# Cosformer attention and a Hyena gate on one core: transposes by DMA, x2 in row tiles of 128, column tiles for the 64-row leftovers

## The chip, the cores and the metric

The kernel runs on one core of a Trainium2 chip. The metric is device time in microseconds (us), the median of several runs. One more execution is profiled; its span, its waits and its durations are what the text below calls the profile.

## The reference

Eight batches, 8 heads, 576 positions (S), 64 features a head; 8 x 64 = 512 channels (DM). All inputs and the output are float32.

```python
# attention: q, k, v are [8, 8, 576, 64]
theta = pi / 2 * arange(576) / 576
phi(x) = concat([relu(x) * cos(theta), relu(x) * sin(theta)], axis=-1)      # 128 features
kv  = einsum('bhsf,bhsd->bhfd', phi(k), v);  z = phi(k).sum(axis=2)
att = einsum('bhsf,bhfd->bhsd', phi(q), kv) / (phi(q) . z + 1e-6)
x   = att, heads side by side: [8, 576, 512]
# gate
x1, x2, x3 = split(x @ w_proj, 3)                      # w_proj [512, 1536]
conv = irfft(rfft(x2, axis=1) * rfft(filter, axis=0))  # along the 576 positions
out  = (x1 * conv * x3) @ w_out                        # [8, 576, 512]
```

## The kernel before

Everything between HBM and PSUM is f16. A load converts while it transfers (issued on GpSimd's queue, POOL): q, k and v arrive as `raw` tiles of 96 partitions, each partition holding six neighbouring positions of all heads; four `raw` buffers take turns. One set of names per batch:

- `emit_phi` (L460, the arithmetic through the helpers at L97 and L99): kp = relu(k) times cos and sin, 12 VectorE operations; qp = relu(q) and relu(q) times tan, 7 operations. The missing cos of a row cancels in the quotient; `epsc` corrects the 1e-6.
- `emit_va` (L125): v into a padded tile, 4 ScalarE copies. `emit_kv` (L485): 48 matmuls, phi(k) as weights.
- `emit_qt` (L499): 48 transposes of 96x96 on TensorE with a permutation matrix `perm`, which brings positions into the order of the later DFT; each PSUM unit is copied into `qpt` twice, forward by VectorE (L511) and backward by ScalarE (L515), as 60 of 64 columns. There is one `qpt` buffer.
- `emit_num` (L520): per head five matmuls of 128 rows (positions from the front in one half, mirrored from the back in the other), a reciprocal, and `att` [128, 5, 512] (L540).
- `emit_fx` (L547): a small matrix `fm` (24 blocks of 10 columns) folds `att` into `fx` [128 channels, 4, 24, 48]. Blocks 0 to 11 are the butterflies of a radix-6 step, blocks 12 to 23 the plain positions, both with channels on partitions. Sixteen matmuls of 240 columns (L556) and four of 192 for the leftover tile (L570).
- `emit_x2` (L584): 3 parts x 2 components x 4 matmuls of 512 columns with 96 rows each, evicted to `x2f` (L598). `emit_dft` (L600): six matmuls with the tables `tre` and `tim` (96x96), then the product with the filter's spectrum on VectorE (L612 to L617).
- `emit_gate` (L619): x1 and x3 directly from the plain blocks of `fx`, 64 matmuls of 288 columns (L630); x1 is evicted by ScalarE (L636), and VectorE multiplies it with x3 from PSUM into `g` (L638).
- `emit_inv` (L647): 32 inverse-DFT matmuls. `emit_y` (L665): additions and the product with g. `emit_out` (L684): five row tiles of 128 (the last from row 448, so 64 rows are computed twice), 20 matmuls of 512 columns (L695), eviction (L700, in the last batch L702 and L97), 9 stores on SyncE's queue (SP), part of them on ScalarE's in the last two batches.

Batches overlap by hand: turn b of the main loop (L801) holds x2, dft, gate and inv of batch b, num and fx of batch b+1, the loads, phi, va, qt and kv of batch b+2, and out of batch b-1. Batches 0 and 1 and the tables (DFT, filter spectrum) are set up ahead of the loop. Each engine takes its instructions in a fixed order, which a scheduler makes from the order of the calls; `with behind(...)` (L109) puts an engine's instructions behind a marked one. All PSUM work shares four units of [128, 2, 512] float32 (L63).

Of the kernel before, what the change touches and what calls it, by code (L numbers as in the profile page):

```python
# [17 lines left out]
def kernel(  # L18
# [15 lines left out]

    nc = tc.nc
# [6 lines left out]
    NT = 5  # L42
# [25 lines left out]
    tcol = consts.tile([128, NJ], FP32, tag="tcol", name="tcol")  # L68
    epsc = consts.tile([128, NT], FP32, tag="epsc", name="epsc")
    perm = consts.tile([NP, NP], FP16, tag="perm", name="perm")  # L70
# [5 lines left out]
    fm = consts.tile([128, 24, 10], FP16, tag="fm", name="fm")  # L76
    tre = consts.tile([NP, 3, NP], FP16, tag="tre", name="tre")
    tim = consts.tile([NP, 3, NP], FP16, tag="tim", name="tim")

# [9 lines left out]
    qpt_buf = [consts.tile([128, NH, NT, 2, 64], FP16, tag=f"qpt{i}", name=f"qpt{i}") for i in range(1)]  # L89
# [24 lines left out]
    raw_t = {}  # L114

    def load_qk(b, nm, hs=slice(0, NH)):
        src = {"q": q, "k": k, "v": v}[nm]
        if hs.start == 0:
            rw = work.tile([NP, NH, NJ * D], FP16, tag="raw", bufs=4, name=f"{nm}raw{b}")
            raw_t[(b, nm)] = rw  # L120
        nc.gpsimd.dma_start(
            out=raw_t[(b, nm)][:, hs], in_=src[b, hs].rearrange("h (p j) d -> p h (j d)", j=NJ)
        )

    def emit_va(b, xs=range(4)):  # L125
        for x in xs:
            hs = slice(2 * x, 2 * x + 2)
            nc.scalar.copy(  # L128
                out=va_buf[b % 2][:, hs, :, 0:D],
                in_=raw_t[(b, "v")][:, hs].rearrange("p h (j d) -> p h j d", j=NJ),  # L130
            )
# [28 lines left out]
    def emit_iotas(part):  # L160
# [13 lines left out]
        iota("sr_i", [NP, QS], lambda t: [(t, [[2, 3], [12, NP // 2]], 1, 0)])  # L174

    def emit_cols():
# [6 lines left out]
        nc.vector.memset(warm, 0.0)  # L183
        sj = cc["s6_i"]
# [3 lines left out]
        nc.vector.tensor_tensor(out=tcol, in0=tcol, in1=scol, op=AL.mult)  # L188

        u16 = small("u16p")  # L190
        rnd(u16, p, 1.0 / 16.0, -15.0 / 32.0)
        dest = small("dest")
        tsc(dest, p, 6.0, AL.mult)
        nc.vector.scalar_tensor_tensor(
            out=dest, in0=u16, scalar=-95.0, in1=dest, op0=AL.mult, op1=AL.add
        )
        tsc(perm, cc["nrow_i"], dest[0:NP], AL.is_equal)

    def emit_pads():
        for va in va_buf:  # L200
            nc.vector.memset(va[:, :, :, D : D + 2], 1.0 / A1)
        for t in qpt_buf:
            nc.vector.memset(t[:, :, :, 0, 60:64], 0.0)
            nc.vector.memset(t[:, :, :, 1, 0:4], 0.0)

    def emit_fm():

        p = cc["p"]
        loc = small("loc")
        side = small("side")  # L210
        nc.vector.tensor_copy(out=loc[0:64], in_=p[0:64])
        tsc(loc[64:128], p[64:128], -1.0, AL.mult, 127.0, AL.add)
        nc.vector.memset(side[0:64], 1.0)
        nc.vector.memset(side[64:128], -1.0)
        lo = small("lo")
        rnd(lo, loc, 1.0 / 6.0, -5.0 / 12.0)
        li = small("li")
        nc.vector.scalar_tensor_tensor(
            out=li, in0=lo, scalar=-6.0, in1=loc, op0=AL.mult, op1=AL.add
        )  # L220


        orb = small("orb", NT)
        for t in range(NT):
            tsc(orb[:, t : t + 1], lo, 10.0 * t, AL.add)
        oj = small("oj", NT)
        rnd(oj, orb, 1.0 / 16.0, -15.0 / 32.0)
        pos = small("pos", NT)

        tsc(pos, orb, 6.0, AL.mult)  # L230
        nc.vector.scalar_tensor_tensor(
            out=pos, in0=oj, scalar=-95.0, in1=pos, op0=AL.mult, op1=AL.add
        )
        nc.vector.scalar_tensor_tensor(
            out=pos, in0=li.to_broadcast([128, NT]), scalar=96.0, in1=pos, op0=AL.mult, op1=AL.add
        )
# [6 lines left out]
        orow_i = cc["orow_i"][:, 0:10]  # L243
        match = small("match", 10)
# [5 lines left out]
        for sl, (kk, c0) in enumerate([(0, 0.25), (3, 0.25), (1, 0.25), (1, 0.0), (2, 0.25), (2, 0.0)]):  # L250
# [4 lines left out]
        nc.scalar.activation(out=coef[:, 0:6], in_=ph, func=AF.Sin, scale=TWO_PI)  # L255
        tsc(coef[:, 3:6:2], coef[:, 3:6:2], 1.0 / R3, AL.mult)

        tsc(coef[:, 0:6], coef[:, 0:6], 2.0, AL.mult)
        tsc(coef[:, 0:6], coef[:, 0:6], RC, AL.add, -RC, AL.add)
        tsc(coef[:, 0:6], coef[:, 0:6], 0.5, AL.mult)  # L260
        tsc(coef[:, 6:12], coef[:, 0:6], side, AL.mult)
# [12 lines left out]
            in0=coef.unsqueeze(2).to_broadcast([128, 24, 10]),  # L274
            in1=match.unsqueeze(1).to_broadcast([128, 24, 10]),
# [23 lines left out]
    def emit_rows():  # L299
# [5 lines left out]
        par = cc["par"] = small("par")  # L305
        rnd(par, p, 0.5, -0.25)
        nc.vector.scalar_tensor_tensor(
            out=par, in0=par, scalar=-2.0, in1=p, op0=AL.mult, op1=AL.add
        )
# [10 lines left out]
    def emit_fwd_tables():  # L320
# [4 lines left out]
        u = small("u16")  # L325
        rnd(u, p, 1.0 / 16.0, -15.0 / 32.0)
        j = small("jr")
        nc.vector.scalar_tensor_tensor(
            out=j, in0=half, scalar=-3.0, in1=u, op0=AL.mult, op1=AL.add
        )  # L330
        w = small("w2s")

        tsc(w, p, 12.0, AL.mult, 1.0, AL.add)
        nc.vector.scalar_tensor_tensor(out=w, in0=u, scalar=-192.0, in1=w, op0=AL.mult, op1=AL.add)
        nc.vector.scalar_tensor_tensor(out=w, in0=j, scalar=2.0, in1=w, op0=AL.mult, op1=AL.add)
# [24 lines left out]
        for tb in (tre, tim):  # L360
            tsc(tb[:, 1:3], tb[:, 1:3], amp[0:NP], AL.mult)
            nc.vector.tensor_tensor(out=tb[:, 0], in0=tb[:, 0], in1=mask, op=AL.mult)

# [59 lines left out]
    def emit_h():  # L423
        hc, hs_, hb, alt = cc["hc"], cc["hs"], cc["hb"], cc["alt"]
        fa = filt16.rearrange("p x (j n) -> p x j n", j=3)
        for x, op in ((0, AL.add), (1, AL.subtract)):
# [5 lines left out]
        for bl in range(3):  # L432
# [15 lines left out]
            tsc(h3[:, bl, 1], u[0:NP, 1], sc, AL.mult)  # L448
            nc.vector.tensor_copy(out=h3[:, bl, 2], in_=h3[:, bl, 1])
        u = unit("h_nyq")  # L450
        for j in range(3):
            nc.tensor.matmul(
                u[0:1, 0], alt[:, j % 2 : j % 2 + 1], feo[:, 0, j], start=(j == 0), stop=(j == 2)
            )
        nc.scalar.activation(out=h3[0:1, 0, 2], in_=u[0:1, 0], func=AF.Copy, scale=1.0 / S)
# [4 lines left out]
    def emit_phi(b, nm, h0=0, nh=NH):  # L460
        rw = raw_t[(b, nm)]
        dst = kp_t if nm == "k" else qp_t
        if h0 == 0:
            dst[b] = work.tile([NP, NJ, NH, 2, D], FP16, tag=f"{nm}p", bufs=2 if nm == "q" else 1, name=f"{nm}p{b}")
        t = dst[b]
        if nm == "q":

            tsc(
                t[:, :, h0 : h0 + nh, 0],
                rw[:, h0 : h0 + nh].rearrange("p h (j d) -> p j h d", j=NJ), 0.0, AL.max,  # L470
            )
        for j in range(NJ):
            for cs, col in ((0, ccol), (1, scol)) if nm == "k" else ((1, tcol),):
                mark["phi", b, nm] = tsc(
                    t[:, j, h0 : h0 + nh, cs], rw[:, h0 : h0 + nh, ds(j * D, D)],
                    col[0:NP, j : j + 1], AL.mult, 0.0, AL.max,
                )
# [21 lines left out]
    def emit_qt(b, hp):  # L499
        qp, qpt = qp_t[b], qpt_buf[0]  # L500
        u = psum.tile([128, 2, 1024], FP16, tag="u", bufs=4, name=f"qt{b}_{hp}")
        for hh in range(2):
            for j in range(NJ):
                nc.tensor.transpose(  # L504
                    u[:, hh, ds(j * NP, NP)],
                    qp[:, j, 2 * hp + hh].rearrange("p a b -> p (a b)"),
                    perm,
                )
        hsl = slice(2 * hp, 2 * hp + 2)
        ev = nc.scalar.copy if b == 0 and hp < 2 else nc.vector.tensor_copy  # L510
        mark["qpt", b, hp] = ev(  # L511
            out=qpt[:, hsl, :, 0, 0:60],
            in_=u[:, :, 0:300].rearrange("p h (t c) -> p h t c", c=60),
        )
        nc.scalar.copy(  # L515
            out=qpt[:, hsl, ::-1, 1, 4:64],
            in_=u[:, :, 276:576].rearrange("p h (t c) -> p h t c", c=60),
        )

    def emit_num(b, hp, wm=0):  # L520
        qpt, kvs = qpt_buf[0], kvs_t[b]
        if hp == 0:
            att_t[b] = work.tile([128, NT, DM], FP16, tag="att", bufs=2, name=f"att{b}")
# [3 lines left out]
        for hh in range(2):  # L527
            h = 2 * hp + hh
            for t in range(NT):
                nc.tensor.matmul(  # L530
                    u[:, hh, ds(t * 65, 65)], qpt[:, h, t].rearrange("p a b -> p (a b)"),
                    kvs[:, h // 4, ds((h % 4) * 65, 65)], start=True, stop=True,
                )
        nv = u[:, :, 0 : NT * 65].rearrange("p h (t e) -> p h t e", e=65)
        rcp = work.tile([128, 2, NT], FP32, tag="rcp", bufs=2, name=f"rcp{b}_{hp}")
        nc.vector.tensor_tensor(
            out=rcp, in0=nv[:, :, :, 64], in1=epsc.unsqueeze(1).to_broadcast([128, 2, NT]), op=AL.add
# [5 lines left out]
            in1=rcp.unsqueeze(3).to_broadcast([128, 2, NT, D]),  # L543
# [3 lines left out]
    def emit_fx(b, cs=range(NC), ccs=None, wm=0):  # L547
        att = att_t[b]
        if 0 in cs:
            fx_t[b] = work.tile([128, NC, 24, 48], FP16, tag="fx", bufs=2, name=f"fx{b}")  # L550
        fx = fx_t[b]
        for c in cs:
            u = unit(f"fx{b}_{c}")
            warm_up(u, wm)
            for t in range(NT - 1):
                nc.tensor.matmul(  # L556
                    u[:, t // 2, 0:480].rearrange("p (g o) -> p g o", o=20)[:, :, ds((t % 2) * 10, 10)],
                    att[:, t, ds(c * 128, 128)], fm, start=True, stop=True,
                )
            nc.scalar.copy(  # L560
# [319 lines left out]
```

## Time and profile before

| | us |
|---|---|
| three runs | 269.84, 270.54, 272.35; median 270.54 |
| the profiled execution | 272.95 |
| its span | 271.2 |
| busy TensorE, VectorE, ScalarE | 243.0, 226.9, 196.8 |

Read it so: the span holds all engines at once, so a busy share near 100% means that an engine is hardly ever without work, and a part removed from another engine moves nothing unless it was waited for. TensorE's matmuls are pipelined, so one record (say 382 ns for 512 columns) is longer than the distance to the next (217 ns). The granted clock of TensorE was 0.978 of full speed on average; it was 0.5 between 66 and 70 us.

### The profile page before, as it was taken

What the parts mean: (1) busy time and instruction counts of PE and PEld (TensorE: products, weight loads), DVE (VectorE), ACT (ScalarE), POOL (GpSimd) and SP (SyncE); (2) the same over time, 40 slices, a digit from 0 to 9 for tenths busy, and PEclk for the clock granted to TensorE, in tenths of its full rate; (3) what the DMA queues carried; (4) which work ended last, traced back from release to release, by engine and by line L of the source; (5) the groups of instructions that cost most, each with busy time, mean ns of one, the idle gap of its engine ahead of it and who ended that gap; (6) DMA issues with size and microseconds to landing.
All of it is one profiled execution on the core that took longest, in us unless ns stands there. A gap on an engine that the chain in (4) does not pass through costs nothing.

```text
span 271.2 us, 6320 instructions
## 1 busy us (share of the span) xinstructions
PE 243.0 (90%) x2457; PEld 175.2 (65%) x2457; DVE 226.9 (84%) x805; ACT 196.8 (73%) x274; POOL 27.3 (10%) x47
## 2 busy tenths in 40 slices
PE   0287998878989999999999999999999999999991
PEld 0164767547858776786678676867687768756830
DVE  7689997998899898979897989978997479646951
ACT  2279679798497778877897789786977667857630
POOL 8551111020020101110111011000000000000000
PEclk9999999995799999999999999999999999999998
DMA  5999998919019296636860868114000600060235
GB/s 79 168 206 205 206 205 122 166 14 169 3 14 161 33 230 90 89 40 152 150 101 3 174 128 124 16 51 125 0 2 9 169 2 0 2 174 13 69 117 155
DMA packets 26991, 26.70 MB, mean 98 GB/s; under 512 B 1680, under 2 KB 22160, under 8 KB 26960
## 3 DMA queue, kind: packets, MB, share of 16 engines
q0 software_dynamic: 21200, 16.84, 42.7%
q1 hardware_dynamic: 5120, 8.39, 10.7%
q10 hardware_dynamic: 640, 1.05, 1.3%
q8 instruction: 19, 0.31, 0.5%
q14 instruction: 12, 0.10, 0.1%
HBM read 33.69 MB, written 9.44 MB: 159 GB/s over the span
## 4 chain that ended last, share of the span: by engine, by line
PE 50%; ACT 22%; DVE 21%; DMA 4%; issue 1%; POOL 0%; SPq 0%; POOLq 0%; ACTq 0%
PE x L630 20%; PE x L593 9%; ACT x2f L598 7%; ACT va L128 7%; PE kv L491 5%; PE out L695 4%; PE fx L556 4%; DVE eo L672 4%; ACT fx L560 3%; DMA vraw<-in_v_dram 2%; DVE kp L99 2%; PE qt L504 2%; PE dft L607 2%; PE inv L657 2%; DVE qpt L511 2%; PE inv L656 2%
## 5 line engine op out<-in xcount | busy, mean ns | idle before, releaser
L630 PE MATMUL x<-fx,wp 128*128 128x288 f16 x512 | 67.5, 286 | 1.1 <-ACT fx L560 1.0
L630 PEld LDWEIGHTS <-wp 128*128 128x128 f16 x512 | 50.0, 98 | 13.3 <-issue 0.3
L593 PE MATMUL x<-wp,fx 128*96 128x512 f16 x192 | 45.2, 382 | 0.5 <-ACT x2f L598 0.5
L560 ACT CAST fx<-fx 128x960 f16<-128x960 f32 x32 | 30.6, 961 | 13.7 <-PE fx L556 13.7
L695 PE MATMUL out<-wo,y 128*128 128x512 f16 x160 | 37.6, 379 | 0.7 <-DVE y L677 0.7
L598 ACT ACTIVATE x2f<-x 96x1024 f16<-96x1024 f32 x24 | 24.5, 1020 | 14.6 <-PE x L593 14.6
L593 PEld LDWEIGHTS <-fx 128*96 128x96 f16 x192 | 22.4, 124 | 15.1 <-issue 0.8
L672 DVE TENSOR_TENSOR eo<-eq 128x144 f16<-128x144 f16 x128 | 23.7, 228 | 10.1 <-ACT eq L660 9.9
L128 ACT COPY va<-vraw 96x768 f16<-96x768 f16 x32 | 25.3, 827 | 9.3 <-DMA vraw<-in_v_dram 9.3
L638 DVE TENSOR_TENSOR g<-x,x1s 128x288 f16<-128x288 f32 x64 | 27.0, 448 | 1.3 <-PE x L630 1.1
L491 PE MATMUL kv<-va,kp 96*128 96x65 f16 x384 | 16.4, 202 | 11.7 <-ACT va L128 8.8
L540 DVE TENSOR_TENSOR att<-num,rcp 128x640 f16<-128x640 f32 x32 | 26.1, 820 | 0.3
L515 ACT COPY qpt<-qt 128x600 f16<-128x600 f16 x32 | 20.4, 671 | 7.5 <-DVE qpt L511 7.5
L695 PEld LDWEIGHTS <-y 128*128 128x128 f16 x160 | 14.9, 97 | 16.0 <-DVE y L677 1.2
L609 ACT CAST xf<-dft 96x1024 f16<-96x1024 f32 x24 | 23.5, 1010 | 2.2 <-PE dft L607 1.2
L491 PEld LDWEIGHTS <-kp 96*128 96x128 f16 x384 | 15.3, 104 | 13.3 <-DVE kp L99 8.1
L504 PEld LDWEIGHTS <-qp 96*128 96x128 f16 x384 | 20.2, 102 | 5.1 <-issue 1.1
L636 ACT CAST x1s<-x 128x576 f16<-128x576 f32 x32 | 20.5, 639 | 4.2 <-PE x L630 3.1
L612 DVE TENSOR_TENSOR m<-xf,h 96x1024 f16<-96x1024 f16 x24 | 16.3, 678 | 7.8 <-ACT xf L609 7.7
L504 PE MATMUL qt<-perm,qp 96*128 96x96 f16 x384 | 21.7, 213 | 0.5 <-ACT fx L560 0.3
L700 ACT ACTIVATE os<-out 128x1024 f32<-128x1024 f32 (+1 forms) x21 | 18.3, 883 | 5.2 <-PE out L695 5.1
L556 PE MATMUL fx<-fm,att 128*128 128x240 f16 x128 | 18.8, 270 | 2.2 <-DVE att L540 1.1
(185 smaller groups left out, 419.4 us busy)
## 6 DMA issues: line engine op xcount, KB each, us to landing
out_dram<-os SPq DMA_DIRECT2D x22, 192.0 KB, 2.5
qraw<-in_q_dram POOLq DMA_DIRECT2D x7, 576.0 KB, 6.6
kraw<-in_k_dram POOLq DMA_DIRECT2D x7, 576.0 KB, 6.3
vraw<-in_v_dram POOLq DMA_DIRECT2D x7, 576.0 KB, 6.5
out_dram<-os SPq DMA_DIRECT2D x20, 128.0 KB, 2.4
wp<-in_moe_w_proj_dram POOLq DMA_DIRECT2D x3, 512.0 KB, 12.3
out_dram<-os SPq DMA_DIRECT2D x22, 64.0 KB, 2.1
kraw<-in_k_dram POOLq DMA_DIRECT2D x2, 288.0 KB, 6.4
```

Of the source, the lines that this page charges most:

```text
L128: nc.scalar.copy(out=va_buf[b % 2][:, hs, :, 0:D], in_=raw_t[(b, "v")][:, hs].rearrange("p h (j d) -> p h j d", j=NJ),)
L491: nc.tensor.matmul(u[:, h // 4, ds((h % 4) * 65, 65)], kp[:, j, h].rearrange("p a b -> p (a b)"), va[:, h, j, 0:65], start=(j == 0), stop= ...
L504: nc.tensor.transpose(u[:, hh, ds(j * NP, NP)], qp[:, j, 2 * hp + hh].rearrange("p a b -> p (a b)"), perm,)
L540: mark["att", b, hp] = nc.vector.tensor_tensor(out=att[:, :, ds(hp * 128, 128)].rearrange("p t (h d) -> p h t d", h=2), in0=nv[:, :, :, 0: ...
L556: nc.tensor.matmul(u[:, t // 2, 0:480].rearrange("p (g o) -> p g o", o=20)[:, :, ds((t % 2) * 10, 10)], att[:, t, ds(c * 128, 128)], fm, s ...
L560: nc.scalar.copy(out=fx[:, c, :, 0:40].rearrange("p g (u o) -> p u g o", u=2), in_=u[:, :, 0:480].rearrange("p u (g o) -> p u g o", o=20),)
L593: nc.tensor.matmul(u[0:NP, comp], fx[:, c, ds(comp * 6 + 2 * bl, 2)].rearrange("p a b -> p (a b)"), wp16[:, c, ds(DM, DM)], start=(c == 0) ...
L598: mark["x2f", b, bl] = nc.scalar.mul(out=x2f[:, bl], in_=u[0:NP], mul=X2SC)
L630: nc.tensor.matmul(u[:, hf, 0:HS], wp16[:, i, ds(w * DM + c * 128, 128)], fx[:, i, ds(12 + 6 * hf, 6)].rearrange("p a b -> p (a b)"), star ...
L638: mark["g", b, c] = nc.vector.tensor_tensor(out=(g[:, c, 0:HS] if hf == 0 else g[:, c, HS:S][:, ::-1]).rearrange("p (j i o) -> p j i o", j ...
L672: nc.vector.tensor_tensor(out=eoh[:, a, :, ds(48 * x, 48)], in0=eqj[:, a, 0], in1=eqj[:, a, 1], op=op)
L695: nc.tensor.matmul(u[:, x], y[:, c, ds(OT[t], 128)], wo16[:, c], start=(c == 0), stop=(c == NC - 1),)
```

## The change

1. *Transposes by DMA.* From batch 2, q is loaded by three DMAs instead of one, so that positions of a pair of partitions swap places in the second half of the features' columns (`DMA_QT = 2`); `emit_phi` then makes qp in a layout with 96 blocks of 128 columns, and four DMA transposes on SP's queue write `qpt` whole. For batches 0 and 1 TensorE still transposes, with an identity and a swap matrix, and each unit is evicted once (one head by ScalarE, one by VectorE).
2. *The gate's operand.* From batch 1 a DMA transpose of `att` gives `xt` [128 channels, 6, 4, 96], and the gate reads it; `fx` keeps only the 12 butterfly blocks. In batch 0 a second fold makes `xt`.
3. *Positions in six tiles of 96* instead of five of 128: `att` is [96, 6, 512], `fm` has blocks of 8 columns, and 48 num matmuls and 24 fold matmuls of 96 columns take the place of 40, 16 and 4.
4. *x2 in row tiles of 128.* The 576 rows of `fx` are cut in four tiles of 128 and one of 64. The 64-row tile is computed in both 64-column halves of the array, two channel groups each. The DFT tables no longer meet the tiles' edges, so seven padded tables `tpad` of 128 rows are filled by eight DMAs on SP, and dft has nine matmuls.
5. *Gate.* ScalarE evicts x3 too (`x3s`), and VectorE multiplies two f16 tiles. eo is made in 8 operations of 288 instead of 16 of 144.
6. *out.* The last tile is rows 512 to 575, computed as two half-width pieces in the two column halves. Stores are cut at multiples of 48 or 96 rows: 14 a batch. In the last batch each tile has its own unit and its own buffer (`osl`, 5), evictions are cut between VectorE and ScalarE, the tiles are taken in the order 1, 0, 2, 4, 3, and stores alternate between SP and ScalarE's queue.
7. *Order.* dft is split in its three parts and interleaved with num, x2 and gate; two of the four va copies go to VectorE from batch 3; phi of q comes earlier, phi of k later; h and x2 of batch 0 are placed differently, y of batch 0 moves into turn 1, and two parts of x2 of batch 1 move ahead of the loop. The two copies of h that VectorE made from PSUM go to ScalarE.

The core of the diff:

```diff
+        if nm == "q" and b >= DMA_QT:
+            nc.gpsimd.dma_start(out=rw[:, hs, 0 : 3 * D], in_=view[:, :, 0 : 3 * D])
+            for x in range(2):
+                nc.gpsimd.dma_start(
+                    out=rw[x::2, hs, 3 * D : 6 * D], in_=view[1 - x :: 2, :, 3 * D : 6 * D])
...
 def emit_qt(b, hp):
+        if b >= DMA_QT:
+            nc.sync.dma_start_transpose(
+                out=qpt[:, hsl].rearrange("p h (j n) -> p (h j) n", j=NJ),
+                in_=qp[:, hsl].rearrange("p h j a b -> p (h j a b)"))
+            return
...
+    def emit_xt(b):
+        xt_t[b] = work.tile([128, NT, NC, NP], FP16, tag="xt", bufs=2, name=f"xt{b}")
+        nc.sync.dma_start_transpose(
+            out=xt_t[b].rearrange("p t c n -> p (t c) n"),
+            in_=att_t[b].rearrange("p t n -> p (t n)"))
...
 def emit_num(b, hp, wm=0):
+                m = NP if hh and t >= 4 else 128
+                c0 = h * S + 2 * NP * (t // 2) + t % 2
                 nc.tensor.matmul(
-                    u[:, hh, ds(t * 65, 65)], qpt[:, h, t].rearrange("p a b -> p (a b)"),
+                    u[0:m, hh, ds(t * 65, 65)], qpt[:, c0 : c0 + 2 * m - 1 : 2],
...
 def emit_x2(b, bls=range(3)):
+            if bl < 2:
+                for x in range(2):
+                    for c in range(NC):
+                        mm(u[:, x], 2 * bl + x, 128, c, range(NC))
+            else:
+                for c in range(2):
+                    for x in range(2):
+                        mm(u[ds(64 * x, 64), 0], 4, 64, c + 2 * x, range(2 * x, 2 * x + 2))
...
+    DFT = (
+        ((tre[:, 0], 0),), ((tpad[0], 0), (tpad[1], 1)), ((tpad[2], 1), (tpad[3], 2)),
+        ((tpad[4], 2),), ((tre[:, 2], 3),), ((tpad[5], 3), (tpad[6], 4)),
+    )
...
 def emit_gate(b, c):
-                        fx[:, i, ds(12 + 6 * hf, 6)].rearrange("p a b -> p (a b)"),
+                        xt[:, i, ds(6 * hf, 6)].rearrange("p a b -> p (a b)")
+                        if b < DMA_XT else xt[:, :, i, ds(48 * hf, 48)],
...
+        if b < 2 or c in X3_ACT:                       # X3_ACT = (0, 1, 2, 3): always
+            nc.scalar.copy(out=x3s, in_=us[1][:, :, 0:HS])
...
 def emit_out(b, grps=OG):
+                if t == 4 and not last:
+                    for c in range(NC):
+                        for hf in range(2):
+                            nc.tensor.matmul(
+                                u[ds(64 * hf, 64), x, 0 : DM // 2], y[:, c, 512:576],
+                                wo16[:, c, ds(hf * (DM // 2), DM // 2)],
+                                start=(c == 0), stop=(c == NC - 1))
```

## The prediction

> **What bounds the kernel now.** I read the page's busy times and slices first, to see which engine is never idle.
>
> ```profile
> PE 243.0 (90%) x2457; PEld 175.2 (65%) x2457; DVE 226.9 (84%) x805; ACT 196.8 (73%) x274; POOL 27.3 (10%) x47
> ...
> PE   0287998878989999999999999999999999999991
> ...
> DVE  7689997998899898979897989978997479646951
> ...
> PEclk9999999995799999999999999999999999999998
> ```
>
> From slice 12 on TensorE is full. Before that (up to some 70 us) VectorE is the fuller one, and between 62 and 71 us the granted clock is 0.5. The chain of waits starts its kv matmuls at 99.08, 127.58, 156.08, 184.58 and 213.08 us, so one batch costs 28.5 us. Next the busy time by stretch, one for each turn of the batch loop (b = 1, 2, 5, 6, then 7 and 8):
>
> ```profile
> 71.43:100.76 29.33, 28.30 (x304) 20.72 (x303) 26.88 (x89) 23.19 (x31) 2.42 (x3) 0.99 0.55 96
> 100.76:129.27 28.51, 27.90 (x304) 20.67 (x302) 25.77 (x85) 23.04 (x31) 2.48 (x3) 1.00 0.59 99
> ...
> 186.27:214.76 28.49, 27.89 (x303) 20.67 (x302) 24.16 (x81) 22.99 (x31) 0.00 (x0) 1.00 0.13 35
> 214.76:239.17 24.41, 24.17 (x208) 17.07 (x206) 17.69 (x56) 17.25 (x22) 0.00 (x0) 1.00 0.08 24
> 239.17:271.20 32.03, 25.28 (x166) 15.51 (x164) 17.36 (x56) 15.50 (x22) 0.00 (x0) 0.98 0.36 106
> ```
>
> Columns: length, busy PE, PEld, DVE, ACT, POOL, clock, DMA share, GB/s. Where DVE falls from 25.77 to 24.16 and DMA from 0.59 to 0.13, the turn keeps its length: TensorE sets it. Matmul durations overlap, so I price by the distance from one start to the next:
>
> ```profile
> 222.75 2.12 PE L630 MATMUL x<-fx,wp 128*128 128x288 f16 x16
> ...
> 224.71 0.57 PE L556 MATMUL fx<-fm,att 128*128 128x240 f16 x4
> ...
> 225.12 2.12 PE L630 MATMUL x<-fx,wp 128*128 128x288 f16 x16
> ```
>
> 16 gate matmuls take 1.96 us, 4 folds 0.41. Read the same way: 8 matmuls of 512 columns 1.73, 12 transposes of 96 columns 0.51, 20 num matmuls 0.61, 48 kv 1.69, one inv matmul 0.0625. A turn before: gate 7.84, x2 5.2, out 4.33, fold 1.64 + 0.33, dft 1.3, qt 2.04, kv 1.69, inv 2.0, num 1.22: 27.6. The other 0.9 of 28.5 are short waits.
>
> **The change, part by part (one turn).**
>
> *TensorE.* qt goes to the DMA queue: -2.04. The fold makes 24 matmuls of 96 columns; priced as the 96-column transposes, 24 x 0.0425 = 1.02: -0.95. num has 48 instead of 40: +0.24. dft has 9 instead of 6 matmuls of 512: +0.65. x2 has 16 full matmuls and 4 on 64 columns of the array: 3.47, plus 0.87 if those run one by one or 0.43 if in pairs: -0.87 to -1.3. out likewise has 16 plus 8 half-width ones of 256 columns, 0.87 or 0.43: 0 to -0.43. Together -3.0 to -3.8. No row shows two halves of the array at work, so I take the middle, -3.4, which leaves 24.2. The gate's moving operand becomes six blocks of 48; no row reads one so, and I price it as the contiguous 288 (bounds: 0, and 64 x 0.008 = 0.5 us, 0.008 being what a 65-column kv matmul takes over its columns' share of 217 ns per 512). The new order puts num and x2 between x2f's eviction and the dft that needs it, where the third dft now waits 0.3, so I keep 0.8 of waits: a period of 25.0, **3.5 less**.
>
> The Trainium skill, "TensorEngine Tiling (Array Packing)", Feature Incompatibilities, says that column tiling turns fast weight load off, which speaks against the 64-column pieces. The loads of 96 columns here take 123 ns against 98 for 128 columns, and both lie under a 217 ns matmul; by the rule the pieces cost perhaps 0.1 us more a turn, by the rows nothing.
>
> *VectorE and ScalarE.* They must fit under 25.0. The groups of the turn from 129.27 to 157.76 (busy us, mean ns of one, idle before):
>
> ```profile
> L638 DVE TENSOR_TENSOR g<-x,x1s 128x288 f16<-128x288 f32 x8 | 3.4, 447 | 0.0
> ...
> L515 ACT COPY qpt<-qt 128x600 f16<-128x600 f16 x4 | 2.5, 668 | 1.6 <-DVE qpt L511 1.6
> ...
> L511 DVE COPY qpt<-qt 128x600 f16<-128x600 f16 x4 | 1.8, 464 | 0.0
> ...
> L675 DVE TENSOR_TENSOR y<-eo 128x288 f16<-128x288 f16 x4 | 1.2, 306 | 0.0
> ```
>
> On VectorE, start to start: the qpt copies go, 4 x 0.39 = -1.56. g reads two f16 tiles in SBUF and is priced as y: 8 x (0.37 - 0.215) = -1.24. eo is 8 of 288 elements instead of 16 of 144: 8 x 0.215 - 16 x 0.145 = -0.6. att has 768 elements instead of 640: 4 x 0.13 = +0.5. Two va copies arrive, +0.6. The relu of q in two: +0.05. Sum -2.2; 25.7 becomes 23.5. On ScalarE: qpt -2.5; fx 576 elements for 960 and no fxc, -4 x 0.32 - 0.8; x2f -0.45; two va copies -1.5; out's last piece -0.3; x3s 4 x 0.64 = +2.6. Sum -4.2; 23.0 becomes 18.8. Both fit, VectorE with 1.5 us to spare.
>
> *Queues.* Each turn SP now issues four transposes of 288 KB (qt), one of 576 KB (xt) and 14 stores instead of 9. SP goes in order: three qt wait for qp and for num's reads of the single qpt buffer, xt waits for att, then the fourth qt, then the stores. Who waits: num of the next turn for qt, gate of the next turn for xt, and ScalarE's next os eviction for the stores; behind that eviction stand kvs and x2f, and so TensorE.
>
> ```profile
> L715 SPq DMA_DIRECT2D out_dram<-os x64: 314/447/1550, 95.6 to 267.3; - x64
> ```
>
> A store's issue takes 0.45 us (least, median and most are given in ns); the list of DMAs has size and us to landing:
>
> ```profile
> out_dram<-os SPq DMA_DIRECT2D x22, 192.0 KB, 2.5
> ...
> wp<-in_moe_w_proj_dram POOLq DMA_DIRECT2D x3, 512.0 KB, 12.3
> ```
>
> No row shows a DMA transpose. Bounds for 1728 KB a turn, one landing before the next: at the store's 192 KB in 2.5 us, 22.5 us if nothing overlaps; at wp's 512 KB in 12.3 us, 41.5. From below, five transfers in flight together cost one landing of some 6.6 us (the 576 KB loads). Stores are issued 0.45 us apart and land after 2.5, so transfers of this very queue do overlap; I take the store's price with half of it overlapped, some 11 us, which with 14 x 0.45 = 6.3 us of stores fits into 25. A turn of slack hides it: cost 0. If that cover went, each us beyond 25 would lengthen a turn by one.
>
> The Trainium skill, "Advanced Engine Details and Errata", X-Bar Transpose (TRN2), expects 350 to 400 GB/s for these, an estimate of 4.4 to 5.1 us a turn. Against it, "VectorE: DVE Perf Modes", The three transpose paths, gives 1309 ns for one 128x128 block by DMA and 390 on TensorE; if the 72 blocks of a turn went singly that would be an estimated 94 us and the kernel would more than double. No row of this trace decides between them.
>
> q's load becomes three DMAs on POOL, two more issues of 0.77 us on an engine that is 10% busy, and half as long packets: at most twice 6.6 us. It is issued about a turn ahead, so 0; if late, relu stands on VectorE with eo and y behind it.
>
> *The start (to 100.76).* VectorE limits it. Removed: batch 2's qpt copies -1.56, h's three evictions -2.1, g(0) -1.24. Added: att(0) and att(1) +1.0, small set-up operations and seven memsets some +1.3. That is -2.6, and turn 1 saves -2.2 more on VectorE (y(0) moves into it, x2(1)'s first parts out of it): **-5**, between -2 and -9 (a longer stretch at half clock, or TensorE's full share). The eight small table copies on SP land near 30 us, dft(0) is past 45.
>
> *Turn 6* has no qt: fold -0.95, num +0.24, x2 -1.1, dft +0.65, out -0.2: **-1.3**.
>
> *The end.* In the chain of waits the last evictions wait for a buffer (start, us, what):
>
> ```profile
> 261.61 2.06 DMA out_dram<-os
> 263.67 0.60 ACT os L702
> ...
> 265.02 1.89 DMA out_dram<-os
> 266.91 0.69 DVE os L97
> ```
>
> From the last y (261.46) to the end are 9.7 us. With a buffer for each tile: 3.0 us of matmuls, half an eviction 0.45, and the 3.6 that now follow the last eviction: 7.1, so -2.6. x2 -1.1, dft +0.65, out -0.2, g and eo on VectorE -0.9, x3s ahead of the last g +0.6: **-3.5**.
>
> **Sum** against the profiled 272.95 (span 271.2 and 1.75 around it): -5 - 4 x 3.5 - 1.3 - 3.5 = -23.8, or 249.2. The median of the runs is 2.4 below the profiled one: **247 us**. Bounds: -2 - 4 x 2.2 - 0.5 - 1.5 = -12.8 and -9 - 4 x 4.2 - 1.8 - 5 = -32.6, so 238 to 258.
>
> **Rivals.** *VectorE becomes the bound* (0.16). For it: 23.5 of 25.0 us, and the start shows it full. If g keeps its 0.37 in spite of f16 and the va copies cost 0.46 each, it has 25.1; at the present share of busy time (25.7 of 28.5) a turn is 27.8. Then -3 - 4 x 0.7 - 0.5 - 3.5 = -9.8: 261. Against it: y's row has g's very shape.
>
> *The transposes set the period; slower* (0.11). Place: the SP queue. Beside 6.3 us of stores they may take 22.2 us in a turn of 28.5: at 78 KB/us the gain is gone, below that it is a loss. At wp's 41.6 KB/us a turn is 47.8 and six of them add 116: about 380 us. For it: the serial store price, 22.5, stands just at this point. Against it: stores do not run singly, and a turn's slack lies ahead of both consumers. Right at the point the time is unchanged (0.04).
>
> *The change gains nothing on TensorE in the turns*, since weight loads with a step of two in num and half-array switches eat 2 us (0.05): -5 - 6 - 0.5 - 3 = -14.5, 256.
>
> **How the numbers follow.** My forecast has 0.64; faster by over 1% holds 0.64 + 0.16 + 0.05 = 0.85, within 1% 0.04 and slower 0.11 (1% is what this measurement can tell from no change). The range goes from 239 to 259: the forecast's own bounds, the last rival and the better half of VectorE's; some 0.2 stays outside.
>
> **What would show it.** Right: periods of 24.5 to 25.5 us with PE over 95%, no DVE qpt rows, g near 0.3 us, SP waiting for qp and os rather than num or gate for DMA. Wrong: num or gate idle behind the transposes or os behind a store (the slower rival), DVE full with PE gaps, x2's 64-column pieces at 0.2 us each, a head that still ends after 97 us, or a last store chain longer than 7 us.

## The result, and the profile after: 291.1 us, slower

The changed kernel takes 291.1 us (median of four runs, 286.4 to 293.2), the kernel before 271.1 beside it (269.8 to 272.4): a ratio of 1.062, 95% interval 1.049 to 1.074. All ratios here take only the executions within 1.5% of their kernel's shortest (of the changed kernel the two at 286.4 and 289.2 us, some 17 us over the kernel before), and the profiled execution of the changed kernel, 293.02 us with a span of 291.2, is not among them. Those two had spans of 284.6 and 287.4. The busy times and slices of its page:

```profile
PE 224.9 (77%) x2309; PEld 153.5 (53%) x2309; DVE 213.4 (73%) x747; ACT 176.7 (61%) x271; POOL 35.3 (12%) x61
...
PE   0388979986169999991599907998999999959700
...
PEclk9997999999859999998599986999999999997965
...
q1 hardware_dynamic: 51470, 20.18, 50.0%
```

TensorE has 18 us less work than before and is idle in four places: holes at slices 11, 19 and 24, and the end. After each hole the granted clock is low as well. q1, the queue of SP's stores and transposes, went from 10.7% to 50.0% of the DMA engines' time. By turns (columns: length, busy PE, PEld, DVE, ACT, POOL, clock, DMA share, GB/s):

```profile
66.90:102.59 35.69, 24.64 (x286) 17.44 (x283) 25.09 (x83) 19.38 (x30) 2.81 (x5) 0.86 1.12 138
102.59:126.80 24.21, 24.21 (x270) 17.07 (x269) 23.86 (x76) 19.15 (x28) 3.54 (x5) 1.00 1.12 126
126.80:162.71 35.91, 26.13 (x270) 17.72 (x269) 24.14 (x77) 19.20 (x28) 3.55 (x5) 0.86 1.12 142
162.71:197.25 34.54, 25.74 (x270) 17.55 (x269) 23.81 (x76) 19.20 (x28) 1.54 (x2) 0.90 1.09 138
...
247.00:291.20 44.20, 24.76 (x162) 15.06 (x159) 16.21 (x45) 15.60 (x23) 0.00 (x0) 0.82 0.28 78
```

The undisturbed turn is 24.21 us with TensorE 100% full: the work is as small as forecast. Its neighbours with the same work take 35, and the end 44.2 for before's 32.0. The chain of waits names what was waited for (start, us, what):

```profile
129.81 12.02 DMA qpt<-qp
...
163.94 12.83 DMA qpt<-qp
...
244.01 7.13 DMA out_dram<-os
...
251.81 8.19 DMA out_dram<-os
...
260.11 1.03 ACT os L829
```

num waits for q's transposes in turns 3 and 4. At the end SP's next issue waits for a store of 96 rows, issued at 244.01, that lands after 7.1 us. ScalarE's eviction then waits for a store of 32 rows that SP issued at 251.81, right behind another one of 96, and that lands after 8.2. In the kernel before a store of 96 rows took 2.5 us to land.

### The profile page after: what moved, and what is told of

Read it like the earlier page. It is cut to its first block, busy times and chain, and to the rows that moved or that the text cites. A ratio compares the mean times of both kernels' runs of the same rounds, so it can differ in the third digit from the quotient of the medians.

```text
span 291.2 us, 6141 instructions
## 1 busy us (share of the span) xinstructions
PE 224.9 (77%) x2309; PEld 153.5 (53%) x2309; DVE 213.4 (73%) x747; ACT 176.7 (61%) x271; POOL 35.3 (12%) x61
## 4 chain that ended last, share of the span: by engine, by line
PE 57%; DMA 24%; ACT 9%; DVE 3%; issue 1%; ACTq 1%; POOL 0%; SPq 0%; POOLq 0%
PE x L713 21%; DMA qpt<-qp 10%; PE out L785 8%; PE x L648 7%; DMA xt<-att 6%; DMA out_dram<-os 5%; PE dft L680 4%; PE kv L543 3%; PE fx L611 3%; PE num L584 3%; PE inv L750 3%; PE inv L749 3%; ACT va L145 2%; DMA vraw<-in_v_dram 2%; PE qt L563 1%; PE out L803 1%
## 5 line engine op out<-in xcount | busy, mean ns | idle before, releaser
L713 PE MATMUL x<-xt,wp 128*128 128x288 f16 x512 | 70.1, 293 | 12.2 <-DMA xt<-att 8.8
L666 ACT ACTIVATE x2f<-x 128x1024 f16<-128x1024 f32 (+1 forms) x24 | 21.2, 884 | 38.9 <-PE x L648 38.9
L648 PE MATMUL x<-wp,fx 128*128 128x512 f16 (+1 forms) x160 | 36.5, 394 | 2.3 <-DVE qpt L569 1.6
L584 PE MATMUL num<-kvs,qpt 128*128 128x65 f16 (+1 forms) x384 | 18.0, 202 | 21.4 <-DMA qpt<-qp 19.5
L738 DVE TENSOR_TENSOR g<-x3s,x1s 128x288 f16<-128x288 f16 x64 | 17.6, 300 | 21.4 <-ACT x3s L723 21.4
L594 DVE TENSOR_TENSOR att<-num,rcp 96x768 f16<-96x768 f32 x32 | 30.4, 949 | 0.4
L785 PE MATMUL out<-wo,y 128*128 128x512 f16 (+1 forms) x132 | 30.3, 379 | 0.0
L723 ACT CAST x3s<-x 128x576 f16<-128x576 f32 x32 | 20.4, 638 | 8.8 <-PE x L713 7.6
L626 ACT CAST fx<-fx 128x576 f16<-128x576 f32 x32 | 20.2, 640 | 5.4 <-PE fx L611 5.4
L753 ACT CAST eq<-inv 128x576 f16<-128x576 f32 x32 | 18.4, 672 | 0.8 <-PE inv L750 0.8
```

Of the source, the lines that this page charges most:

```text
L584: nc.tensor.matmul(u[0:m, hh, ds(t * 65, 65)], qpt[:, c0 : c0 + 2 * m - 1 : 2], kvs[:, h // 4, ds((h % 4) * 65, 65)], start=True, stop=True,)
L594: mark["att", b, hp] = nc.vector.tensor_tensor(out=att[:, :, ds(hp * 128, 128)].rearrange("p t (h d) -> p h t d", h=2), in0=nv[:, :, :, 0: ...
L626: mark["fx", b] = nc.scalar.copy(out=dst[:, c].rearrange("p g (j o) -> p j g o", j=3), in_=uf[:, 0:768].rearrange("p (j g o) -> p j g o", ...
L648: nc.tensor.matmul(dst, fx[:, c].rearrange("p g o -> p (g o)")[:, ds(128 * ch, n)], wp16[:, c, ds(DM, DM)], start=(c == cs[0]), stop=(c == ...
L666: mark["x2f", b, bl] = nc.scalar.mul(out=x2f[:, 2 * bl : 2 * bl + n], in_=u[:, 0:n], mul=X2SC)
L713: nc.tensor.matmul(u[:, hf, 0:HS], wp16[:, i, ds(w * DM + c * 128, 128)], xt[:, i, ds(6 * hf, 6)].rearrange("p a b -> p (a b)") if b < DMA ...
```

## The experiments

The theories, as they came up: **A**, the transposes' own throughput against the loads; **B**, their place in SP's queue and the single qpt buffer; **C**, the other parts lose by themselves; **D**, the shape of the new stores; **E**, the order of the transposes. Medians are of four runs (both_split ten), ratios against the kernel before.

### Which transposes?

qt_tensor:

```diff
-    DMA_QT = 2
+    DMA_QT = 8
```

> The 24 DMA transposes of q go back to TensorE (48 transposes of 96 columns a batch, one eviction each on ScalarE and VectorE); those of att (7 of 576 KB) stay on SP's queue. Theory A: the DMA transposes are what the changed kernel waits for, as SP's queue and the DMA engines cannot finish 1728 KB of them a turn beside 14 stores and the loads. Then with a third of the bytes the waits of num go, a turn costs the undisturbed 24.2 plus 2.04 for the transposes, 26.3 us, and the time is about 67 + 5 x 26.3 + 24.4 + 36 + 1.8 = 261 us (255 to 266). Theory C: the loss lies in the other parts (row tiles, column pieces, the new tail, the clock): then it stays above 280 us.

(With this edit q's load is one DMA again in every batch.)

xt_tensor:

```diff
-    DMA_XT = 1
+    DMA_XT = 8
...
     def emit_xt(b):
+        if b < DMA_XT:
+            return
```

> The 7 DMA transposes of att go, a second fold on TensorE makes the gate's operand in every batch (+1.0 us a turn, 4 more evictions on ScalarE); the 24 transposes of q stay on SP's queue. Theory A: two thirds of the bytes are left, some 11 of the 17 to 25 us that SP spends on them in a turn, beside 12 of stores; it just fits 25.3 us, num waits little, 255 to 268 us. If only the long transfer's place in the queue mattered (the fourth transpose of q stands behind it), the same. Theory B: the single qpt buffer and the place behind the stores are what makes q's transposes late, whatever the bytes: num still waits some 20 us in all, 270 to 285 us. Theory C: above 285.

both_tensor: both edits.

> No DMA transpose is left; all other parts of the change stay. Theories A and B agree: no wait for a transpose, a turn of 24.2 + 2.04 + 1.0 = 27.3 us, the time about 67 + 1 + 5 x 27.3 + 25.4 + 36 + 1.8 = 268 us (262 to 272), about the kernel before. Theory C: the other parts lose by themselves, 280 or more. It also shows what the end costs without transposes in the queues: 36 us against 44.2 in the changed kernel if the transposes delayed the stores, 44 if the new tail itself is slow.

| | us | ratio |
|---|---|---|
| qt_tensor | 283.8 | 1.048 (1.040 to 1.055) |
| xt_tensor | 285.0 | 1.047 (1.037 to 1.057) |
| both_tensor | 286.4 | 1.058 (1.052 to 1.064) |

All three expectations by A were missed. Without a single DMA transpose the kernel is still 5.8% slower than before, so C, that other parts of the change lose by themselves, holds for a part. both_tensor's turns are 28.2 us, about before's, and its end, from 240 us on, is 45.6. The chain there (lines shift by two in this kernel):

```profile
238.00 1.03 ACT os L831
239.05 7.11 DMA out_dram<-os
...
246.84 8.18 DMA out_dram<-os
...
255.12 1.03 ACT os L831
```

So the slow stores have nothing to do with transposes. The DMA view of that stretch, 248 to 255 us, in 40 slices (share of the 16 engines in tenths, then GB/s), next to the kernel before in its own last part, 238.5 to 248.5 us:

```profile
DMA  2354625523467321111111837631111111111111
GB/s 70 105 141 129 135 70 146 176 70 88 123 176 199 111 70 59 53 70 47 47 47 47 129 82 117 152 106 59 59 47 47 47 47 70 47 41 47 53 47 47
```

```profile
DMA  9894396988489999758910000000000000000000
GB/s 270 246 312 180 98 246 164 246 180 238 156 262 279 279 311 336 279 148 213 213 41 0 0 0 0 0 0 0 0 0 0 0 0 0 0 0 0 0 0 0
```

Long stretches of the first stay at share 1 and 47 GB/s. In both kernels a 2048-byte packet of a store takes 84 ns (the median of the trace's packet records), 24.4 GB/s for one engine. 47 GB/s are two engines. The kernel before keeps some ten at work with packets of the same size.

What differs is the shape. A store of 96 rows was `[96, 512]` in the output; now it is `out=ov[:, m // 2]`, of shape `[2, 48, 512]`. The Trainium skill, "DMA: Bandwidth & Descriptors", section "Why a DMA increments its semaphore by 16 and not by 1", says that a DMA is spread over the largest number of engines up to 16 that divides the slowest dimension of both access patterns. For `[2, 48, 512]` against 96 partitions that is 2, for 48 or 32 rows 16. The rates above agree, and the kept traces settle the number. Where the rate stays at 47 GB/s, exactly two packets of q1 are in flight at a time; in the kernel before it is up to 16. The semaphore that tells of a DMA's landing is counted up in steps: three steps for each of the changed kernel's 24 stores of this shape, one right after the issue and two when data has landed, and sixteen for every other store of both kernels.

The same records show what this does to the other stores. Of 81 stores with sixteen steps on SP's queue in the changed kernel, 70 get the last two more than 1 us after the fourteenth (none of 64 in the kernel before): they have packets on the two engines too, behind the slow stores. So the 8.2 us at the end are those of a store of 32 rows. Its fourteenth step came at 254.46, the last two at 259.60 and 260.00.

### Stores on another queue

stores_act:

```diff
-                    q_ = nc.sync
+                    q_ = nc.scalar
                     if last:
```

> All stores are issued on ScalarE's queue and the DMA transposes have SP's queue to themselves. In the changed kernel SP's cycle from one batch's transposes to the next takes 37.9, 34.4 and 27.7 us, of which 17 to 25 are transposes and 12 to 16 stores with their waits. Theory B (order: the transposes stand behind the stores): the cycle falls to 17 to 25 us, below or near a turn, and the time to 255 to 268 us; ScalarE gets some 6 us more a turn and is still under 25. Theory A in its pure form (the DMA engines' throughput): transposes land as late as before, 282 to 293 us.

331.1 us, 1.221 (1.213 to 1.228): both theories missed. Its waits:

```profile
ACT kvs L549 <- DMA out_dram<-os: 38.2, 5, 11.0
PE num L584 <- ACT kvs L549: 33.0, 4, 12.6
```

ScalarE now stands behind slow stores, and TensorE behind ScalarE. The transposes, alone on SP, are issued in 12 to 14 us a turn from 108 us on; in the changed kernel it is 17 to 25 until its loads end. So another queue does not cure it: a slow store stalls the engine that issues the next ones. The traces show how. The DMAs of the program use eight semaphores in turn, and an issue waits until the DMA that had its semaphore before has landed. In the changed kernel SP issues a store at 107.54 with the semaphore of the one of 99.80, which landed at 107.52; in stores_act ScalarE issues one at 140.22, and the one of 129.98 landed at 140.20.

### The shape of the stores

split cuts each store of 96 rows into two of 48:

```diff
-  e = pos + 96 if pos % 96 == 0 and pos + 96 <= hi_ else min(hi_, (m + 1) * 48)
+  e = min(hi_, (m + 1) * 48)
```

> The changed kernel with one edit: each store of 96 rows (192 KB, three a batch), which goes out with two halves of 48 rows as the outer of three dimensions, is cut in two stores of 48 rows with two dimensions (17 stores a batch for 14). In the changed kernel's records the packets of these stores keep two DMA engines busy (2048-byte packets of 84 ns, 50 KB/us), the stores of before seven to thirteen; the store that the end waits for lands after 7.1 and 8.2 us, and transposes issued behind such stores have 19 packets in flight with next to none finishing for 4 to 6 us. Theory D: this is the loss at the end (two waits of ScalarE's eviction for a store and the last landing, about 15 us) and most of the lateness of the transposes: 291 - 15 - 15 to 30 = 245 to 262 us. Theory A (the transposes' own throughput against the loads): only the end gets shorter, num still waits some 20 us, 274 to 280. Theory B (the number of issues on SP): three more stores, 288 to 296.

both_split has this edit in both_tensor, xt_split in xt_tensor.

> As both_tensor (no DMA transpose at all), with the stores of 96 rows cut in two. Theory D: the end, 45.6 us from 240 us on in both_tensor, where two stores of 7.1 and 8.2 us stand on the chain and 13 us pass after the last issue, falls to about 30; the turns, 28.2 us and set by VectorE and TensorE in turn, stay: 270 us (266 to 276). Theory A or B: the stores are not it and the time stays at 284 to 288.

> As xt_tensor (the gate's operand by a second fold on TensorE, q's transposes by DMA), with the stores of 96 rows cut in two. Theory D: 15 us less at the end and no wait of num (11.5 us in xt_tensor): turns of 24.2 + 1.0 = 25.3 us, 285 - 15 - 11.5 - 2 for the clock = 256 us (251 to 262). If the transposes of q stay late for another reason (the single buffer, the loads), 266 to 272. It also tells whether the DMA transpose of att is worth its bytes: above split it is.

| | us | ratio |
|---|---|---|
| split | 246.0 | 0.894 (0.887 to 0.902) |
| both_split | 271.1 | 0.998 (0.994 to 1.002) |
| xt_split | 251.2 | 0.928 (0.921 to 0.936) |

Theory D in all three. By the ratios one line of code is worth 0.168 of the time before, some 45 us, and split beats both kernels. In split only one of 126 stores on SP gets its last two steps over 1 us after the fourteenth. With the stores repaired the transposes on DMA bring 0.104, some 28 us (both_split against split); without them the turns stay at 28.0 to 28.4. xt_split stands 0.034 above split, so the transpose of att alone is worth some 9 us. The DMA view of both_split for its last part, 237.5 to 247.5 us:

```profile
DMA  0377756416587537484677768330205250030000
...
out_dram<-os SPq DMA_DIRECT2D x9, 96.0 KB, 2.0
```

Each half of a former store of 96 rows lands after 2.0 us. split_cols tests whether the number of stores did it:

```diff
-  q_.dma_start(out=ov[:, m // 2], in_=sv[pos - OT[t] : e - OT[t]])
+  for hf in range(2):
+      q_.dma_start(out=ov[:, m // 2, :, ds(hf * (DM // 2), DM // 2)],
+                   in_=sv[pos - OT[t] : e - OT[t], ds(hf * (DM // 2), DM // 2)])
```

> As the changed kernel, but each store of 96 rows is cut in two by columns: still two halves of 48 rows as the outer dimension, now with packets of 1 KB. So there are 17 stores a batch, as in split, with the two-fold shape of the changed kernel. Theory D (a store whose outermost dimension is 2 is spread over two DMA engines only): it lands as slowly as before and nothing is gained, 285 to 300 us. If only the number or the size of the stores mattered (192 KB in one store against 96), it is as fast as split: 243 to 253.

287.9 us, 1.062 (1.053 to 1.071): as slow as the changed kernel. Seventeen stores of 96 KB or less are slow in one shape and fast in the other, and all 48 column halves show three steps of their semaphore.

### End and turns, and the order

split_last (split_first has `b >= 5` in the same place):

```diff
-  e = pos + 96 if pos % 96 == 0 and pos + 96 <= hi_ else min(hi_, (m + 1) * 48)
+  e = pos + 96 if b < 5 and pos % 96 == 0 and pos + 96 <= hi_ else min(hi_, (m + 1) * 48)
```

> The stores of 96 rows are cut in two by rows in batches 5, 6 and 7 alone, whose stores lie from turn 6 on; SP's order in the turns is that of the changed kernel (three transposes of q, that of att, the fourth of q). Theory D: the end gains its 15 us, the waits of the gate and num for transposes in turns 1, 3 and 4 stay: 276 us (270 to 280).

> The converse: the stores are cut in batches 0 to 4 alone, the end has the two-fold stores. Theory D: the turns are 24.2 to 25 us, the end keeps some 44 us: 260 us (256 to 267). With split_last the two gains should add up to split's 45 us.

split_last takes 268.7 us, 0.990 (0.982 to 0.997); split_first 266.0, 0.980 (0.972 to 0.987). By the ratios the end is worth 0.072 and the turns 0.082, some 20 and 22 us, together 42 for split's 45. So the two add up, within the noise, as expected. The single figures were off: split_last is 7 us under its 276 and below its range, split_first 6 us over its 260 and inside its range.

In split the scheduler also changed SP's order: att's transpose, then all four of q, instead of three of q, att's, the fourth. xt_first puts that order into the changed kernel:

```diff
+  mark["xt", b] = nc.sync.dma_start_transpose(out=xt_t[b]...
...
+  with behind("xt", n):
       emit_qt(n + 1, x)
```

> The changed kernel with its two-fold stores, but with the transpose of att placed ahead of all four transposes of q on SP's queue, the order that split has (the scheduler chose it there). Theory E: split gained its turns by this order, as the fourth transpose of q no longer stands behind the 576 KB of att's; then the waits of num go and the end stays: 260 us (256 to 268), as split_first. Theory D: the order matters little, the transposes still stand behind stores that two engines carry: 280 to 293 us.

281.2 us, 1.038 (1.028 to 1.049): theory D's figure. The order has a small share at most: 1.038 against the changed kernel's 1.062, and the intervals touch. Turns 2 to 5 take 116.5 us there (from one kv at 89.8 to another at 206.3), 120.0 in the changed kernel, 97.4 in split.

### Why a slow store makes a transpose late

The DMA view of the changed kernel, 150 to 160 us (slices of 0.25 us); three transposes were issued from 148.56 on, right behind the stores:

```profile
DMA  9999111111111111159999902002999943999999
GB/s 207 216 114 51 49 49 49 49 66 49 49 49 49 49 49 49 38 99 285 315 316 220 51 9 11 9 10 52 294 282 298 272 14 76 292 301 203 197 175 184
```

For 3.5 us only two engines move data, then the rate goes to 300 GB/s. The packet records show the other side: 21 transposed packets (256 bytes, median 18 ns) began in that stretch and took 3.6 to 4.0 us each. All end at 154.4, within 0.3 us of the stores' last packets, and the first of the three transposes begins to land at 155.88, after the last store at 154.94. Such groups of 13 to 21 packets over 2 us (the longest 7.6) are in turns 2 to 6 of the changed kernel, of xt_first and of no_loads (below); split has none. The reading that a transpose needs the two engines that still have a store ahead is inferred from this timing, not shown. It is also only one form of the delay: split_cols has no packet over 2 us. There the transposes start later, 13 to 19 us after the batch's first store (10 to 17 in the changed kernel), with SP waiting 18.6 us for earlier stores.

The next two kernels leave out the loads of batches 3 to 7 (their output is not the reference's) and show that the delay by itself costs the turns nothing.

no_loads (no_loads_split has split's edit as well):

```diff
     def load_qk(b, nm, hs=slice(0, NH)):
+        if b >= 3:
+            raw_t[(b, nm)] = raw_t[(2, nm)]
+            return
```

> The changed kernel with its two-fold stores, without the loads of q, k and v from batch 3 on (batches 3 to 7 use the raw tiles of batch 2, so their output is not the reference's). In the changed kernel the fourth transpose of q takes 12 us to land while loads run (the transposes then move 45 to 80 KB/us, alone 130 to 170). Theory D alone: the stores on two engines hold the transposes up anyway, turns 3 and 4 keep most of their 20 us, 280 to 290 us. Theory A beside it: the loads are the other half, num's waits go and only the end stays slow, 262 to 274 us.

> As split, without the loads of q, k and v from batch 3 on (batches 3 to 7 use the raw tiles of batch 2, so their output is not the reference's). If the loads are what is left of the lateness in split (num's one wait of 8.4 us, and times that spread from 242 to 253), it goes: 236 to 242 us with a narrow spread. If the transposes are late for another reason (their place behind the stores, the single buffer), 243 to 250.

no_loads takes 259.5 us, 0.960 (0.956 to 0.965), SP's order unchanged; no_loads_split 242.4, 0.899 (0.897 to 0.900), its four runs within 0.3 us. That is below the range for no_loads, and at the upper end of the one for no_loads_split. Turns 2 to 5 of no_loads:

```profile
91.35:188.19 96.84, 96.84 (x1078) 68.35 (x1079) 94.69 (x298) 76.61 (x113) 0.00 (x0) 1.00 0.79 120
```

Four turns of 24.2, TensorE full, with the slow stores in place. So it took both: without the slow stores (split) or without the loads (no_loads) the turns are right. The traces suggest how: the stores push the transposes some microseconds back, into the time of the next loads, and beside loads they are slow. The queue lines of the changed kernel for 130 to 140 us (loads running; packets, MB, share), then of split for 104 to 112 us (hardly any):

```profile
q0 software_dynamic: 2083, 1.06, 86.3%
q1 hardware_dynamic: 2165, 0.55, 56.0%
```

```profile
q1 hardware_dynamic: 4753, 1.19, 107.0%
q0 software_dynamic: 21, 0.02, 2.5%
```

0.55 MB in 10 us against 1.19 in 8: 55 KB/us against 149. Loads and transposes together move 161, little more than the transposes alone. By the ratios split (0.894) does not differ from no_loads_split (0.899). Two of split's four runs took 249.0 and 252.6 us, though, and none of the other's over 242.5. That this spread comes from the same meeting is likely but not shown, as split's profile is of a run of 243.0 us.

### An attempt to go further

split_two_qpt, on top of split; the loads, phi and transposes of q are also emitted at the head of the turn, which puts the transposes ahead of att's on SP:

```diff
-    qpt_buf = [... for i in range(1)]          # used as qpt_buf[0]
+    qpt_buf = [... for i in range(2)]          # used as qpt_buf[b % 2]
...
-            dst[b] = work.tile([NP, NH, NJ, 2, D], FP16, tag="qp", bufs=2, ...)
+            dst[b] = work.tile([NP, NH, NJ, 2, D], FP16, tag="qp", bufs=1, ...)
```

> As split, with two qpt buffers (and one qp buffer for two, so the space stays) and the four transposes of q ahead of that of att on SP's queue; nothing else moves on any engine. In split the transposes of q wait on SP for att of the batch before, start some 13 us after the stores' first issue and land 2 to 8 us before or after num wants them: the one wait left is num's 8.4 us in turn 4. Theory D (enough room once the stores run on all engines): they start 3 to 5 us earlier, that wait goes or halves, 238 to 245 us against split's 246. If the single buffer had been no limit, no change; if att's transpose, now last, comes late for the gate, 248 to 256.

Missed: 259.2 us, four runs from 248 to 261, too scattered for an interval. In the profiled run, of 257.7 us, the saved qp buffer has a price:

```profile
DVE qp L105 <- DMA qpt<-qp: 15.0, 4, 7.0
```

VectorE now waits until the transposes have read qp. Two landings of qpt, 7.4 and 3.7 us, also stand on the chain; how much either costs is open.

## Why the prediction was wrong

The span cut at the same kv matmuls in all three profiles: to batch 3's kv, four turns, turn 6, the end.

```profile
100.95 1.63 PE kv L543 x48
...
220.95 1.63 PE kv L543 x48
```

```profile
89.60 1.63 PE kv L543 x48
...
186.98 1.63 PE kv L543 x48
```

(The changed kernel, in its profiled execution of 293.02 us, then split, of 243.01; before 99.08 and 213.08. The end begins at 247.0, 211.2 and 239.17.)

| part | forecast | changed kernel | split |
|---|---|---|---|
| start | -5 | +1.9 | -9.5 |
| four turns | -14 | +6.0 | -16.6 |
| turn 6 | -1.3 | 0.0 | -1.9 |
| end | -3.5 | +12.2 | -2.0 |
| sum | -23.8 | +20.0 | -30.0 |

**The step that failed** is the pricing of the stores under "Queues" and "The end". The prediction counted 14 stores instead of 9 and gave each the old rows' 0.45 us of issue and 2.5 us to landing. It did not look at the shape of the 96-row stores, though the new `rearrange` stands in the diff's `emit_out`. They land 6.6 to 13.8 us after their issue (24 stores, median 8.7; 2.1 to 3.4 before). As an estimate from packets, 48 x 84 ns on each of two engines is 4.0, plus the two or so that a small store takes anyway; the next such store often stands behind it on the same two engines. From a batch's first store to the first transpose SP needs 10 to 17 us in place of 6.3. That turned the end from -3.5 into +12.2 and took from the transposes the time they were given. The skill's rule cited above gives the two engines, and the prediction did not use that page.

**The second failed step** is "a turn of slack hides it: cost 0" for the transposes. Their own size was right: some 11 us a turn were taken, 1728 KB at 149 KB/us are some 12 (an estimate from 8 us of split). The 350 to 400 GB/s that the Trainium skill's "Advanced Engine Details and Errata", X-Bar Transpose (TRN2), expects are not met here: 149 GB/s is the mean, 316 the best slice of 0.25 us in the view above. But the sum put only stores beside them, not the 1728 KB of loads that use the same 16 engines in the same turn; beside those they fall to 55 KB/us. The slack of a turn covers one of the two burdens (no_loads; split), not both.

**The rival** "the transposes set the period; slower" named the right consumers: num and the gate, and ScalarE's os behind a store. Its price was wrong: a rate under 78 KB/us held only beside the loads (55), not for all of a turn's transposes, and the loss was about a fifth of what its 380 us point says (20 of 107).

**Right**, as split shows: a TensorE turn of 24.2 before waits; VectorE under it (24.0 busy, forecast 23.5); ScalarE 19.2 (18.8). g takes 300 ns, as y's row had said. Turn 2 of split, with the columns of the turns above:

```profile
91.23:115.44 24.21, 24.21 (x270) 17.09 (x269) 24.04 (x77) 19.16 (x28) 3.55 (x5) 1.00 1.03 177
```

The pieces for two column halves, from split's chain:

```profile
210.63 0.56 PE out L803 x8
...
215.40 0.55 PE x L648 x4
```

They take 0.55 us for x2 and 0.56 for out, between the forecast's 0.43 for pieces in pairs and 0.87 for one by one, and nearer to the former; their weight loads take 108 to 109 ns against 98 for 128 columns. The 0.8 us of waits that was kept in the period did not come. **VectorE as the bound** is not seen in split. In both_split, with the qpt copies back on it, VectorE operations stand on the chain of the 28.2 us turn, but TensorE is busy 27.2 of 28.0 us and VectorE 25.2, so it is not shown to be the bound there either.

**The start** was better than forecast (-9.5 with the stores repaired, just past the far bound of -9). The +1.9 of the changed kernel holds a wait of 8.8 us for att's first transpose, ahead of any slow store. split_last, with the same order up to there, does not have it (kv at 89.3), so it seems to belong to that execution; its cause is open.

## What to carry to other kernels

When a change rearranges a DMA's access pattern, price it by its outermost dimension and not only by its bytes: here the outer 2 of `[2, 48, 512]` cost some 45 us, and cutting the transfer in two got them back. Such a transfer also holds up the others of its queue. A flat low GB/s figure in the DMA view, at a share of 1 tenth, is how it looks in a profile. Work moved to a DMA queue must be summed with everything that uses the same engines in that turn, loads included, before its cost is called hidden.

## What the hardware showed that was not expected

- A DMA transpose behind a two-engine store can have packets in flight for 3.6 to 4.0 us, once 7.6, whose median is 18 ns.
- DMA transposes between SBUF tiles run at 149 KB/us when nearly alone and at 55 KB/us beside loads that themselves move 106.
- A store on two engines delays the stores on sixteen behind it: fourteen of a store's sixteen landing steps came by 254.46, the last two at 259.60 and 260.00.
